# Second mixture of experts: parts of the work at the joins placed inside the branches, the down matmuls with 512 columns, the weight splits on VectorE in halves

## Chip, cores and metric

The kernel runs on one core of a Trainium2 chip. The metric is the device time of one execution in microseconds, lower is better; the median of several runs is quoted. The engines are named as in the profile: PE (TensorE, its weight loads are PEld), DVE (VectorE), ACT (ScalarE), POOL (GpSimd) and SP (SyncE, which issues most of the transfers). A name with a q behind it, as ACTq, is the engine's sequencer, with its branches and semaphore instructions.

## The reference

Three stages, in float32. A chunked linear attention gives 3072 rows of 256. Then two mixtures of experts follow, of which the change touches the second:

```python
# first mixture: 4 experts, every token goes through all of them
out += p[:, e:e+1] * (relu(x @ w1[e]) @ w2[e])           # w1: 256x1024, w2: 1024x256

# second mixture: 8 experts, each token goes to one, 768 places for each expert
expert_idx = argmax(x @ w_gate, axis=1)
gate_w = softmax(x @ w_gate)[token, expert_idx]
h = relu(disp[e] @ w1[e])                                # disp[e]: the tokens of expert e, in their order
y = h @ w2[e]
out[i] = gate_w[i] * y[expert_idx[i], pos[i]]            # 0 for a token that found no place
```

With the inputs of the measurement the experts get 836 (of which 768 have a place), 313, 184, 362, 215, 164, 196 and 802 (768) tokens.

## The kernel before

Attention, first mixture and routing are interleaved by hand up to about 607 us. The routing writes each token's row, with its gate and its index behind the 256 values, to `disp` in HBM, at its place in its expert. From there the second mixture runs expert by expert; it is this part that the change edits.

**Precision.** A float32 product is made of three matmuls: each operand is split into a high part in fp32r and the rest (h and l in the names), and h·h, h·l and l·h are summed in PSUM. For weights, `split_w` does it: ACT copies a stage of 128x1024 to the high part (L371), and DVE or POOL subtracts it to get the low part (L372). An expert has four such stages, c = 0 to 3, two for w1 and two for w2.

**A block.** `expert_block` runs one block of n = 256 (NARROW) or 384 (SLOTS) tokens of an expert, two or three token tiles of 128. For f = 0 to 7 the up part (`up_part`, L725 to L727) makes 128 of the 1024 hidden values for all n tokens in six matmuls; ACT puts relu of it into `ring_hh` (L729), and DVE the rest into `ring_hl` (L730). The ring has three such pairs. Two f's later (LAG) the down part takes the pair, for each token tile with three matmuls of 256 columns, into one PSUM tile per token tile (L763 to L765). At the block's end ACT scales each sum by the gate (`yo`, L773), and POOL scatters it to `out` by an indirect DMA (L774). Between the steps `go()` runs what the caller has put into `extra`: loading the next expert's rows, transposing them (`turn`, L695, with a copy of the gates, `gi`, on POOL, L697), splitting the transposed rows (`turned`, L703 and L704), loading weight stages and splitting the weights of expert e + 2, at steps 4, 6, 8 and 10. The splits of c = 1, 2 are on DVE, those of c = 0, 3 on POOL.

**The order of the experts.** The counts of tokens are read into registers, and `tc.If` chooses on every engine. For expert 0 the block of 384 always runs, and a second block if it has more than 384 tokens. For each further expert `head(e)`, the up part of f = 0, 1, 2 for the first 256 tokens (18 matmuls), is written ahead of the branches, since every choice has it. Behind it come a branch that runs a block of 256 (`wide{e}`, taken for up to 256 tokens), and one (`over{e}`) that holds a block of 384 (`full{e}`) and a pair of blocks (`next{e}`). At the end of a branch each engine raises the semaphores by what the path that was not chosen would have raised, so that what comes behind counts the same on both paths; the rows of L1090, L1093 and L1097 on the engines' sequencers are the branches and these updates. [...] Expert 7 has its Ifs nested, and behind it stands `redo_first`, a repetition of expert 0's block for other counts, which does not run here (L1063).

So the blocks that run are 384 + 384 for experts 0 and 7, 384 for 1 and 3, and 256 for 2, 4, 5 and 6: 26 token tiles.

```python
for e in range(1, E2):
    tokens = counts[e]
    head(e)
...
    with tc.If(tokens <= NARROW, label=f"wide{e}", preferred_fallthrough_block=True):   # L1090
        hint(f"over{e}")
        first_block(e, NARROW)
    with tc.If(tokens > NARROW, label=f"over{e}", preferred_fallthrough_block=True):    # L1093
```

## Time and profile before

| | us |
|---|---|
| median of 3 runs | 791.07 (789.83 to 792.62) |
| the profiled execution | 795.09 |
| its span, from the first to the last instruction | 793.3 |
| PE busy | 766.5 (97%) |
| DVE, ACT, POOL busy | 440.8 (56%), 282.9 (36%), 189.0 (24%) |
[...]

A span is what the profiler saw of one execution; the profiled execution's own time is 1.8 us longer, and 4.0 us over the median of the runs. Matmuls are pipelined, and the time shown for one is modelled, longer than the distance to the next one's start; idle time ahead of a matmul is counted from the modelled end of the one before. The granted clock is the share of full speed that the chip gave to PE.

### The profile page before, as it was taken

How to read it: one execution, taken by the hardware profiler on the slowest of the kernel's cores; microseconds unless marked ns; L12 is line 12 of the kernel's file. 1: busy time of each engine (PE TensorE's matmuls, PEld its weight loads, DVE VectorE, ACT ScalarE, POOL GpSimd, SP SyncE). 2: the span in 40 equal slices, each digit the busy share in tenths (PEclk: the TensorE clock that was granted, in tenths of full speed). 3: DMA queues.
4: the chain of work that ended last, by engine and by line, in shares of the span. 5: the costliest groups of instructions: out<-in, count | busy, mean ns of one | idle time of the engine just before them, and what ended most of it. 6: DMA issues, size and time to landing. Idle time of an engine off the chain costs nothing. (4 is left out here: it accounts for less than half of the span.)

```text
span 793.3 us, 13459 instructions
## 1 busy us (share of the span) xinstructions
PE 766.5 (97%) x5114; PEld 685.7 (86%) x5114; DVE 440.8 (56%) x884; ACT 282.9 (36%) x555; POOL 189.0 (24%) x227
## 2 busy tenths in 40 slices
PE   8999999999999999999999999999999989998996
PEld 7889999988878888888888888889999989897995
DVE  5886778457754577645666456543444323546321
ACT  2542543232323332233332323322453334555331
POOL 1010102212111122110221103011765313654211
PEclk9999999999999999999999999999999999999999
DMA  9753567523220232201322112040353214453100
GB/s 261 246 174 104 183 213 226 165 84 103 80 83 14 71 110 83 83 14 67 111 84 83 46 52 96 14 143 12 117 163 107 75 44 144 141 169 109 43 21 23
DMA packets 50195, 82.54 MB, mean 104 GB/s; under 512 B 5104, under 2 KB 35009, under 8 KB 50108
## 3 DMA queue, kind: packets, MB, share of 16 engines
q1 hardware_dynamic: 46340, 74.50, 30.0%
q0 software_dynamic: 2400, 6.11, 2.1%
q10 hardware_dynamic: 1368, 0.81, 0.4%
q8 instruction: 50, 0.82, 0.4%
q14 instruction: 37, 0.30, 0.1%
HBM read 65.56 MB, written 16.31 MB: 103 GB/s over the span
## 5 line engine op out<-in xcount | busy, mean ns | idle before, releaser
L502 DVE SCALAR_TENSOR_TENSOR hl<-ph,hh 128x512 fp32r<-128x512 f32 (+2 forms) x216 | 133.9, 620 | 221.7 <-ACT hh L501 218.1
L501 ACT ACTIVATE hh<-ph 128x512 fp32r<-128x512 f32 (+2 forms) x216 | 117.4, 543 | 348.4 <-PE ph L498 337.6
L496 PE MATMUL ph<-xh,w1h 128*128 128x512 f32 (+2 forms) x432 | 160.7, 372 | 1.6 <-DVE hl L502 1.6
L525 PE MATMUL acc<-hh,w2h 128*128 128x512 f32 (+2 forms) x432 | 158.1, 366 | 2.3 <-DVE x L541 1.4
L497 PE MATMUL ph<-xl,w1h 128*128 128x512 f32 (+2 forms) x432 | 156.4, 362 | 0.0
L498 PE MATMUL ph<-xh,w1l 128*128 128x512 f32 (+2 forms) x432 | 156.4, 362 | 0.0
L526 PE MATMUL acc<-hl,w2h 128*128 128x512 f32 (+2 forms) x432 | 156.3, 362 | 0.0
L527 PE MATMUL acc<-hh,w2l 128*128 128x512 f32 (+2 forms) x432 | 156.1, 361 | 0.0
L525 PEld LDWEIGHTS acc<-hh,w2h 128*128 128x128 f32 x432 | 81.2, 188 | 13.9 <-DVE x L541 2.2
L496 PEld LDWEIGHTS ph<-xh,w1h 128*128 128x128 f32 x432 | 81.3, 188 | 12.5 <-DVE hl L502 2.3
L730 DVE SCALAR_TENSOR_TENSOR ring_hl<-qh,ring_hh 128x384 fp32r<-128x384 f32 (+2 forms) x82 | 38.5, 472 | 95.8 <-ACT ring_hh L729 88.3
L498 PEld LDWEIGHTS ph<-xh,w1l 128*128 128x128 f32 x432 | 81.2, 188 | 10.5
L527 PEld LDWEIGHTS acc<-hh,w2l 128*128 128x128 f32 x432 | 81.3, 188 | 10.4
L526 PEld LDWEIGHTS acc<-hl,w2h 128*128 128x128 f32 x432 | 81.3, 188 | 9.4
L497 PEld LDWEIGHTS ph<-xl,w1h 128*128 128x128 f32 x432 | 81.3, 188 | 8.7
L549 POOL TENSOR_TENSOR x<-x,cmb 128x512 f32<-128x512 f32 (+2 forms) x40 | 48.5, 1234 | 153.0 <-DVE cmb L546 152.9
L729 ACT ACTIVATE ring_hh<-qh 128x384 fp32r<-128x384 f32 (+2 forms) x82 | 34.9, 425 | 83.8 <-PE qh L727 81.0
L765 PE MATMUL yy<-w2h,ring_hl 128*128 128x256 f32 x208 | 59.8, 287 | 0.0
L763 PE MATMUL yy<-w2h,ring_hh 128*128 128x256 f32 x208 | 59.7, 287 | 0.0
L764 PE MATMUL yy<-w2l,ring_hh 128*128 128x256 f32 x208 | 59.7, 287 | 0.0
L180 DVE TENSOR_TENSOR_SCAN lt<-abc,id 128x512 f32<-128x512 f32 x44 | 57.4, 1304 | 0.0
L725 PE MATMUL qh<-sxh,w1h 128*128 128x256 f32 (+2 forms) x132 | 42.0, 318 | 10.8 <-DVE ring_hl L730 3.0
(166 smaller groups left out, 1080.8 us busy)
## 6 DMA issues: line engine op xcount, KB each, us to landing
stg<-in_w SPq DMA_DIRECT2D x34, 512.0 KB
abc<-a_zero SPq DMA_DIRECT2D x21, 512.0 KB
bcr<-in_bc SPq DMA_DIRECT2D x19, 512.0 KB
disp<-zrow SPq DMA_DIRECT2D x12, 516.0 KB
nat<-in_nat SPq DMA_DIRECT2D x24, 256.0 KB
pb<-pT SPq DMA_DIRECT2D x16, 256.0 KB
rw<-disp SPq DMA_DIRECT2D x10, 387.0 KB
out<-zrow SPq DMA_DIRECT2D x6, 512.0 KB
```

The source lines that it names most:

```text
L180: nc.vector.tensor_tensor_scan(t["lt"][:, sl, :].rearrange("p h i -> p (h i)"), a_bc[:, sl, :].rearrange("p h i -> p (h i)"), id4.rearrang ...
L496: nc.tensor.matmul(ph[:, :n], lhsT=wh[:, c], rhs=xh[:, k, :n], start=k == 0, stop=False)
L497: nc.tensor.matmul(ph[:, :n], lhsT=wh[:, c], rhs=xl[:, k, :n], start=False, stop=False)
L498: nc.tensor.matmul(ph[:, :n], lhsT=wl[:, c], rhs=xh[:, k, :n], start=False, stop=k == KD - 1)
L501: nc.scalar.activation(hh[:, :n], ph[:, :n], AF.Relu)
L502: nc.vector.scalar_tensor_tensor(hl[:, :n], ph[:, :n], 0.0, hh[:, :n].bitcast(F32), ALU.max, ALU.subtract)
L525: nc.tensor.matmul(a[:, :n], lhsT=wh[:, c], rhs=hh[:, :n], start=f == 0, stop=False)
L526: nc.tensor.matmul(a[:, :n], lhsT=wh[:, c], rhs=hl[:, :n], start=False, stop=False)
L527: nc.tensor.matmul(a[:, :n], lhsT=wl[:, c], rhs=hh[:, :n], start=False, stop=f == NF - 1)
L763: nc.tensor.matmul(y[st], lhsT=hh[:, q], rhs=w2h[:, c], start=j == 0, stop=False)
L764: nc.tensor.matmul(y[st], lhsT=hh[:, q], rhs=w2l[:, c], start=False, stop=False)
L765: nc.tensor.matmul(y[st], lhsT=hl[:, q], rhs=w2h[:, c], start=False, stop=j == NF - 1)
```

## The change

- **Down part.** `w2h` and `w2l` become one tile `w2` of 128 x 2 x 2048. For each token tile and f a matmul of 512 columns multiplies `ring_hh` with both parts, into a PSUM tile of 128 x 2 x 256, and one of 256 columns adds `ring_hl` times the high part to its first half. At the end ACT scales the first half, and DVE adds the second half times the gate (L798), ahead of the scatter. Three such PSUM tiles are made once and used in rotation.
- **Splits.** In the second mixture's blocks all weight splits go to DVE, in halves of 512 columns, at steps m and m + 1.
- **gi.** The copy of gates and indices goes from POOL to DVE, in two instructions at the end of `turned`.
- **Joins.** `head(e + 1)` is no longer in front of the branches but written into every path that leads there, at the end or in the Else. Where the narrow branch isn't taken, its Else holds `first_down`: the down part of f = 0 and 1 for two token tiles. The repetition of expert 0 moves ahead of expert 1, its jump gets a hint ("again"), and expert 7's Ifs stand one behind the other.
- **Alignment.** JOIN becomes 0, and a slot of its own (FIRST_BLOCK) is given to expert 0's block.

```diff
@@ split_w
+    def split_w(moe, e, c, lo, part=slice(0, FF)):
...
+        sl = slice(FF * (c % 2) + part.start, FF * (c % 2) + part.stop)
+        st = given[moe, e, c][:, part]
         nc.scalar.copy(h[:, sl], st)
         lo.tensor_tensor(l[:, sl], st, h[:, sl].bitcast(F32), ALU.subtract)
@@ turn, turned
-        nc.gpsimd.tensor_copy(gi[e, k], rows[:, :, DM:ROW])
...
+        rows, g = whole["rows", e % 2 if k == 0 else 2], gi[e, k]
+        nc.vector.tensor_copy(g[:, :, 0:1], rows[:, :, DM:DM + 1])
+        nc.vector.tensor_copy(g.bitcast(I32)[:, :, 1:2], rows.bitcast(I32)[:, :, DM + 1:ROW])
@@ the down part
+    def down_part(e, y, q, j):
+        w2 = W[2, e][4]
+        hh, hl = ring[j % len(ring)]
+        c = slice(DM * j, DM * j + DM)
+        nc.tensor.matmul(y, lhsT=hh[:, q], rhs=w2[:, :, c], start=j == 0, stop=False)
+        nc.tensor.matmul(y[:, 0], lhsT=hl[:, q], rhs=w2[:, 0, c], start=False, stop=j == NF - 1)
...
+    def first_down(e, y):
+
+        for j in range(LAG):
+            for st, t in enumerate(y):
+                down_part(e, t, slice(P * st, P * st + P), j)
@@ expert_block
-                    nc.tensor.matmul(y[st], lhsT=hh[:, q], rhs=w2h[:, c], start=j == 0, stop=False)
-                    nc.tensor.matmul(y[st], lhsT=hh[:, q], rhs=w2l[:, c], start=False, stop=False)
-                    nc.tensor.matmul(y[st], lhsT=hl[:, q], rhs=w2h[:, c], start=False, stop=j == NF - 1)
+                    if st >= len(early[1]) or j >= lead:
+                        down_part(e, y[st], q, j)
...
-            nc.scalar.activation(o, y[st], AF.Copy, scale=g[:, st, 0:1])
+            nc.scalar.activation(o, y[st][:, 0], AF.Copy, scale=g[:, st, 0:1])
+            nc.vector.scalar_tensor_tensor(o, y[st][:, 1], g[:, st, 0:1], o, ALU.mult, ALU.add)
@@ first_block
-            add(m, lambda w=order[i], lo=(nc.vector if c in (1, 2) else nc.gpsimd): split_w(2, *w, lo))
+            add(m, lambda w=order[i]: split_w(2, *w, nc.vector, slice(0, FF // 2)))
+            add(m + 1, lambda w=order[i]: split_w(2, *w, nc.vector, slice(FF // 2, FF)))
@@ the branches
+    def choose(cond, label, yes, no):
+        with tc.If(cond, label=label, preferred_fallthrough_block=True) as choice:
+            yes()
+        if no:
+            with choice.Else():
+                no()
+
+    def full_program(e, tokens, y):
+        first_block(e, SLOTS, y, LAG, two=True)
+        second_into(e, tokens)
+        head(e + 1)
+        if e + 1 < E2:
+            align(JOIN)
+
+    def wide_programs(e, tokens, y, after):
...
+        choose(tokens <= SLOTS, f"full{e}", lambda: first_block(e, SLOTS, y, LAG, over=f"next{e}"), None)
+        choose(tokens > SLOTS, f"next{e}", lambda: full_program(e, tokens, y), after)
+
+    def narrow_program(e, y):
+        hint(f"over{e}")
+        first_block(e, NARROW, y, 0)
...
+        with tc.If(counts[0] > SLOTS, preferred_fallthrough_block=True):
+            hint("again")
+            second_into(0, counts[0])
+    choose(numbers["known"] < SLOTS, "again", first_once_more, lambda: head(1))
 
     for e in range(1, E2):
...
+        after = (lambda: head(e + 1)) if e + 1 < E2 else None
+        y = [sums(e, 0, st) for st in range(NARROW // P)]
+        choose(tokens <= NARROW, f"wide{e}", lambda: narrow_program(e, y), lambda: first_down(e, y))
+        choose(tokens > NARROW, f"over{e}", lambda: wide_programs(e, tokens, y, after), after)
```

**An expert's end on PE.** The place is the end of expert 1's second block. Before, the last down matmuls (yy; the columns are the row's number, the line, the operation, output and inputs, and the shape) are followed by the alignment (ISA) and the jumps, and then by expert 2's head (qh), which is there once, for all paths:

```order
3628 L763 MATMUL yy_1_2_7421<-w2h_1_5954,ring_hh_6304 128x256
3629 L764 MATMUL yy_1_2_7421<-w2l_1_5955,ring_hh_6304 128x256
3630 L765 MATMUL yy_1_2_7421<-w2h_1_5954,ring_hl_6305 128x256
3631 L785 ISA
3632 L1097 UNCONDITIONAL_BRANCH x2
3633 L1093 UNCONDITIONAL_BRANCH
3634 L725 MATMUL qh_0_0_7549<-sxh_5932,w1h_2_6134 128x256
```

Now the head comes directly behind the last down matmul of this path, with the alignment and the jump behind its 18 matmuls. Behind the jump the same 18 matmuls stand again, for the path without a second block:

```order
3606 L749 MATMUL yy_6377<-w_2_1_5947,ring_hh_6295 128x512
3607 L750 MATMUL yy_6377<-w_2_1_5947,ring_hl_6296 128x256
3608 L733 MATMUL qh_0_0_7611<-sxh_5925,w1h_2_6127 128x256
3609 L734 MATMUL qh_0_0_7611<-sxl_5926,w1h_2_6127 128x256
...
3624 L734 MATMUL qs_0_2_7629<-sxl_5926,w1h_2_6127 128x256
3625 L735 MATMUL qs_0_2_7629<-sxh_5925,w1l_2_6128 128x256
3626 L810 ISA
3627 L1080 UNCONDITIONAL_BRANCH
3628 L733 MATMUL qh_0_0_7639<-sxh_5925,w1h_2_6127 128x256
```

The head (qh, qs) moved from behind the paths' meeting to ahead of it, into each path, and three down matmuls became two.

**The splits on DVE in a narrow block.** Before, in expert 4's block of 256 tokens (ring_hl is L730, the split of the low parts of w1 and w2 L372, the turned rows L704):

```order
880 L730 SCALAR_TENSOR_TENSOR ring_hl_6301<-qh_0_3_9023,ring_hh_6300 128x256
881 L372 TENSOR_TENSOR w1l_2_6135<-stg_3_3_6243,w1h_2_6134 128x1024
882 L730 SCALAR_TENSOR_TENSOR ring_hl_6305<-qh_0_4_9040,ring_hh_6304 128x256
883 L372 TENSOR_TENSOR w2l_2_6137<-stg_4_0_6268,w2h_2_6136 128x1024
884 L730 SCALAR_TENSOR_TENSOR ring_hl_6309<-qh_0_5_9058,ring_hh_6308 128x256
885 L730 SCALAR_TENSOR_TENSOR ring_hl_6301<-qh_0_6_9085,ring_hh_6300 128x256
886 L704 TENSOR_TENSOR sxl_6299<-tr_0_0_9074,sxh_6298 128x384
```

And now in the same block:

```order
1045 L378 TENSOR_TENSOR w1l_2_6128<-stg_3_3_6235,w1h_2_6127 128x512
1046 L738 SCALAR_TENSOR_TENSOR ring_hl_6296<-qh_0_4_9125,ring_hh_6295 128x256
1047 L378 TENSOR_TENSOR w1l_2_6128<-stg_3_3_6235,w1h_2_6127 128x512
1048 L378 TENSOR_TENSOR w_2_2_6129<-stg_4_0_6260,w_2_2_6129 128x512
1049 L738 SCALAR_TENSOR_TENSOR ring_hl_6300<-qh_0_5_9143,ring_hh_6299 128x256
1050 L378 TENSOR_TENSOR w_2_2_6129<-stg_4_0_6260,w_2_2_6129 128x512
1051 L378 TENSOR_TENSOR w_2_2_6129<-stg_3_0_6091,w_2_2_6129 128x512
1052 L738 SCALAR_TENSOR_TENSOR ring_hl_6292<-qh_0_6_9169,ring_hh_6291 128x256
1053 L378 TENSOR_TENSOR w_2_2_6129<-stg_3_0_6091,w_2_2_6129 128x512
1054 L709 TENSOR_TENSOR sxl_6290<-tr_0_0_9159,sxh_6289 128x384
```

The two whole stages on DVE (and two on POOL) became eight halves on DVE, one or two of them between each ring_hl and the next.

**A block's end on DVE.** The yo additions (L798) now stand on DVE between the last ring_hl of a block (f = 7) and the first of the head, as here at expert 3's second block:

```order
1025 L738 SCALAR_TENSOR_TENSOR ring_hl_6296<-qh_1_7_8972,ring_hh_6295 128x384
1026 L798 SCALAR_TENSOR_TENSOR yo_1_0_8999<-yy_6376,gi_6284,yo_1_0_8999 128x256
1027 L798 SCALAR_TENSOR_TENSOR yo_1_1_9005<-yy_6377,gi_6284,yo_1_1_9005 128x256
1028 L798 SCALAR_TENSOR_TENSOR yo_1_2_9011<-yy_6375,gi_6284,yo_1_2_9011 128x256
1029 L738 SCALAR_TENSOR_TENSOR ring_hl_6292<-qh_0_0_9017,ring_hh_6291 128x256
1030 L738 SCALAR_TENSOR_TENSOR ring_hl_6296<-qh_0_1_9026,ring_hh_6295 128x256
```

Before, ring_hl of the head followed directly on ring_hl of f = 7, and yo was ACT's alone.

## Rows read from the trace of the kernel before

**Rows 1.** The page's first part: busy us, share of the span, instructions.

```profile
PE 766.5 (97%) x5114; PEld 685.7 (86%) x5114; DVE 440.8 (56%) x884; ACT 282.9 (36%) x555; POOL 189.0 (24%) x227
```

**Rows 2.** Two stretches: length, busy us and instructions of each engine, PEclk, DMA share, GB/s.

```profile
640.00:660.00 20.00, 17.57 (x122) 17.05 (x121) 5.53 (x11) 7.81 (x16) 5.42 (x5) 0.91 0.23 69
...
700.00:720.00 20.00, 17.00 (x130) 16.35 (x129) 10.59 (x14) 9.28 (x19) 8.87 (x6) 0.95 0.47 147
```

**Rows 3.** PE's waits, 607.6 to 786: releaser: us, times, longest.

```profile
PE qh L725 <- DVE ring_hl L730: 3.6, 4, 1.9
PE qh L725 <- ACTq L1093: 2.7, 4, 0.7
PE qh L725 <- DVEq L1090: 2.0, 2, 1.0
PE qh L725 <- ACTq L1097: 1.4, 2, 0.7
PE qh L725 <- ACT yo L773: 1.4, 1, 1.4
```

**Rows 4.** Timeline of PE at expert 0's end: start, length, operation, [idle before <-releaser].

```profile
645.43 0.28 PE L764 MATMUL yy<-w2l,ring_hh 128*128 128x256 f32 x1
645.55 0.28 PE L765 MATMUL yy<-w2h,ring_hl 128*128 128x256 f32 x1
647.25 0.36 PE L725 MATMUL qh<-sxh,w1h 128*128 128x256 f32 x1 [1.42 <-ACT yo L773]
```

**Rows 5.** Line L785: duration ns min/median/max, first and last start us.

```profile
L785 PEldq COMPARE_BRANCH  x1: 3011/3011/3011, 643.8 to 643.8; - x1
```

**Rows 6.** Line L1093, PE's sequencer, the same columns.

```profile
L1093 PEldq COMPARE_BRANCH  x6: 82/338/358, 649.8 to 747.2; - x6
```

**Rows 7.** Timeline of PE behind a wide branch and behind a join.

```profile
650.63 0.33 PE L725 MATMUL qh<-sxh,w1h 128*128 128x128 f32 x1 [0.99 <-DVEq L1090]
...
669.89 0.38 PE L725 MATMUL qh<-sxh,w1h 128*128 128x256 f32 x1 [0.75 <-ACTq L1097]
```

**Rows 8.** Groups of DVE, 640 to 785 (busy, mean ns), and one of its splits.

```profile
L730 DVE SCALAR_TENSOR_TENSOR ring_hl<-qh,ring_hh 128x256 fp32r<-128x256 f32 x34 | 14.2, 422 | 40.2 <-ACT ring_hh L729 34.6 <-issue 5.5
L704 DVE TENSOR_TENSOR sxl<-tr,sxh 128x384 fp32r<-128x384 f32 x12 | 6.1, 548 | 0.0
L730 DVE SCALAR_TENSOR_TENSOR ring_hl<-qh,ring_hh 128x128 fp32r<-128x128 f32 x9 | 2.6, 292 | 5.8 <-ACT ring_hh L729 5.7
...
692.90 1.23 DVE L372 TENSOR_TENSOR w1l<-stg,w1h 128x1024 fp32r<-128x1024 f32 x1 [0.38 <-ACT w1h L371]
```

**Rows 9.** Timeline of PE and ACT at the last matmul.

```profile
785.15 0.28 PE L765 MATMUL yy<-w2h,ring_hl 128*128 128x256 f32 x1
...
785.47 0.47 ACT L773 ACTIVATE yo<-yy,gi 128x256 f32<-128x256 f32 x1 [0.24 <-PE yy L765]
```

**Rows 10.** Timeline of PE, the first of 15 matmuls and the first behind them.

```profile
652.93 0.42 PE L763 MATMUL yy<-w2h,ring_hh 128*128 128x256 f32 x1
...
656.63 0.28 PE L763 MATMUL yy<-w2h,ring_hh 128*128 128x256 f32 x1
```

**Rows 11.** Timeline of PE in the first mixture, first and last of eleven matmuls.

```profile
299.64 0.39 PE L497 MATMUL ph<-xl,w1h 128*128 128x512 f32 x1
...
301.91 0.39 PE L527 MATMUL acc<-hh,w2l 128*128 128x512 f32 x1
```

**Rows 12.** Timeline of DVE, POOL and PE in expert 4's block.

```profile
712.79 3.36 DVE L372 TENSOR_TENSOR w2l<-stg,w2h 128x1024 fp32r<-128x1024 f32 x1
...
712.70 2.37 POOL L372 TENSOR_TENSOR w2l<-stg,w2h 128x1024 fp32r<-128x1024 f32 x1
...
716.54 0.39 PE L725 MATMUL qh<-sxh,w1h 128*128 128x256 f32 x1 [1.93 <-DVE ring_hl L730]
```

**Rows 13.** Timeline of PE at the second block of expert 0.

```profile
630.62 0.45 PE L725 MATMUL qh<-sh,w1h 128*128 128x384 f32 x1 [0.59 <-DVE ring_hl L730]
```

**Rows 14.** Timeline of POOL at the end.

```profile
787.39 0.98 POOL L774 DMA_INDIRECT out<-yo,gi  x1 [0.30 <-DMA out<-yo,gi]
```

## Prediction

> **What bounds the kernel now.** I read the busy shares first: TensorE (PE) is busy 97% of the span and no other engine over 56% [rows 1], so time can only come from PE's own work or from holes in it. Cutting the span into stretches shows where the holes are: in the second mixture, PE is busy 17.57 of 20 us between 640 and 660 and 17.00 between 700 and 720, and in the same two stretches its granted clock is 0.91 and 0.95 [rows 2]. The list of what PE waited for in 607.6 to 786 names thirteen waits [rows 3]: nine on a branch or a join between experts (ACTq L1093 four, ACTq L1097 two, DVEq L1090 two, and one that is put down to the yo of ACT), 7.5 us, and four on ring_hl of VectorE (DVE), 3.6 us. The change touches nothing ahead of the second mixture but the names of weight tiles and two small copies, so the sum is about the 178 us from 607.6 on.

> **The joins.** After expert 0's last matmul, issued at 645.55, PE starts nothing until 647.25 [rows 4]. The row blames ACT, but the branch on PE's own queue (L785) takes 3011 ns from 643.8 [rows 5], while the six branches of L1093 took at most 358 ns [rows 6]. Those of [rows 6] that jump far have a hint ahead of them, and the one of [rows 5] has none. The change puts a hint ("again") ahead of it, and the head of expert 1 behind it, inside the Else. Eight further holes have one shape: 0.99 us idle ahead of 650.63 at a wide branch, 0.75 ahead of 669.89 at a join [rows 7]. At the end of a branch each engine makes up by semaphore updates for the path that was not taken, and PE's next block waits for those of ACT or DVE, which come behind the rest of their previous block. The change moves head(e+1), 18 matmuls, ahead of that: PE has 18 × 0.12 = 2.16 us of work which needs only PSUM freed by an earlier ring_hl and the turned rows, not the yo. On the wide branch eight matmuls (first_down, 4 × (0.227 + 0.12) = 1.39 us) stand ahead in the same way. The cover is enough: a hole, end to start, is 0.75 to 1.4 us. What becomes late next is DVE, which has the yo additions ahead of the head's first ring_hl; the additions, at about 0.42 us (the ring_hl form of the same shape, [rows 8]), come one behind each token tile, and only the last lies behind PE's last matmul. The last yo of ACT starts 0.32 us after the last matmul and takes 0.47 [rows 9]; with the addition that is 1.2 us, and ring_hl of f=0, which needs its own 0.72 us of matmuls and ACT's hh as well (1.4 us), should be done 1.8 us after it, ahead of the 2.16 us at which first_down wants it.
> What goes: idle of 7.5 us [rows 3], plus 0.16 us for each of nine, because a modelled matmul lasts 0.28 us where the next one starts after 0.12 [rows 4]: 8.95 us. The first matmul after a hole is slower by some 0.1 us, which I leave in. [...] Together **−10.5**. Bounds: nothing regained of the clock (−8.9), and the second, smaller stretch at the low clock around 718 too (−11.6, by the 0.05 × 20 us of [rows 2]).

> **The narrow experts 2, 4 and 5.** Here the splits of expert e+2's weights compete with ring_hl. A DVE split of 1024 columns takes 1.23 us beside an idle POOL [rows 8], but 3.36 us when POOL splits at the same time, and ring_hl behind it then holds PE for 1.93 us [rows 12]. The change takes the POOL splits away and doubles those of DVE. Between ring_hl of f=3 and of f=7 DVE will do 8 halves × 0.65 (half of 1.23 and a little; an estimate from [rows 8]) = 5.2, five ring_hl × 0.42 = 2.1, two sxl × 0.55 = 1.1, two gi copies, each taken at half of the 0.29 us of the smallest form, 0.3: 8.7 us. PE needs, for five f's, six pairs of downs and six transposes, 5 × 0.72 + 12 × 0.347 + 6 × 0.12 = 8.5 us. DVE starts about a microsecond behind and has one pair of downs in reserve, 0.69 us: late by 8.7 + 1.0 − 8.5 − 0.69 = 0.5, and I take 0.65, since DVE also waits a little for ACT in between. In three experts that is 1.95 us, against 3.6 − 0.59 = 3.0 idle now [rows 3, 13], plus 3 × 0.26 for pitch and restart, plus about 1.1 at the lower clock between 700 and 740 (0.05 × 20 us of [rows 2] as the nearest): 4.9. So **−2.9**. Bounds: splits so quick that nothing is late (−4.9); 2.0 us each (+1.1). In experts 1 and 3, of three token tiles, PE has half as much work again and DVE is covered. ACT's casts in halves cost a few tenths per expert, beside other work.

> **Fewer, longer matmuls.** For each of 26 token tiles and 8 f's, two matmuls of 256 columns become one of 512. The down matmuls start every 0.12 us now, and those of 512 columns in the first mixture every 0.227 us, by the first and the last of eleven in a row [rows 11]: 208 × (0.24 − 0.227) = **−2.7**. Bounds: 0 (the two-part operand runs as two of 256) and −2.7.

> **What is added.** (a) The 26 yo additions on DVE, 0.42 each, lie behind a block's end; only at expert 0, where the second block follows with no head between, do they meet something: PE already waits there 0.59 us for ring_hl [rows 13], and three additions are queued ahead of the same ring_hl, of which one is not yet past: **+0.45** (bounds 0 and 1.3). (b) Expert 7 is now two Ifs in a row (full7, next7) in place of nested ones, with no head to cover the drain: a join as it stands now, 2.7 us in four [rows 3]: **+0.7** (bounds 0.5 and, with the stop of [rows 4] in addition, 2.1). (c) The gi copies on DVE: one waits for the scatters that used the same gi. They are a block or more old, so I cost the wait at nothing; if they were late, ring_hl of f=7 would be late by as much. (d) The end: yo is now ACT then DVE, +0.45 ahead of the last scatters, and the wait on L1063 between them goes (0.30 us idle is left ahead of the last scatter, [rows 14]): **0**, bounds −0.5 and +0.5.

> **Sum.** −10.5 − 2.9 − 2.7 + 0.45 + 0.7 = −14.95. The profiled execution took 795.09 us, with a span of 793.3; it is 4.0 us over the median of the runs, 0.5%, more than the runs differ among themselves, so I take the difference from the median: 791.07 − 14.95 = 776.1, and expect a profiled span near 778.4 (793.3 − 14.95). A difference under 0.3%, 2.4 us, could not be told from none.

> **Rivals.**
> 1. *DVE becomes the bound in narrow experts.* ring_hl of f=7 comes 2 us late three times: −2.9 turns into +1.1, and a low-clock stretch of 1.57 follows once: 776.1 + 4.0 + 1.6 = 781.7. For it: DVE's 8.7 us against PE's 8.5. Against: without POOL beside it each split is short [rows 8].
> 2. *The joins stay* with another name: the head's first matmuls wait for the drain after all, because the updates stand in its own instructions. Half of the 8.95 us and all of the 1.57 stay: 776.1 + 6.1 = 782.2. All of both: 786.6.
> 3. *Slower: fetches.* Every jump to another place in PE's program stops as in [rows 5], its hint or alignment having moved. Each costs 1.58 us of hole (1.42 idle + 0.16), and at most 1.57 more at the low clock: about 3.1. It decides from five misses on (14.95 / 3.1 = 4.8); nine, one for each of the old holes, give 776.1 + 28 = 804. For it: the program's order of Ifs, hints and alignment all change. Against: the hinted jumps are quick now [rows 6], and the change keeps the hint ahead of each and adds one. [...]
> 4. *The 512-column matmul is no cheaper.* w2h and w2l lie 2048 columns apart, and the engine reads them as two runs: the 2.7 stays, 778.8. No matmul of the trace has such an operand, for or against; the 512 columns of [rows 11] are one run.

> **How the numbers follow.** My forecast 0.62, rival 1 0.15, rival 2 0.08, rival 3 0.05, rival 4 0.10. The forecast alone covers 772 to 780 by the bounds: −2.0 for the narrow experts and −1.1 for the clock at the low end; +1.3 at expert 7, +0.9 at expert 0 and +1.6 for the clock at the high end. The range of 8 in 10 takes in rivals 1 and 4 and half of rival 2: 771.5 to 783.5. Faster by over 0.3% in all cases but the third, and a little off for all that could stack up: 0.92 faster, 0.04 within 0.3%, 0.04 slower.

> **What would show it.** In the profile after: PE busy 98% or more of a span of about 778; of the nine waits on a branch or join only one of 0.7 us or so at expert 7; no L785-like branch of 3 us; splits of 128x512 on DVE near 0.65 us and none on POOL after 640; the down matmul of 512 columns starting 0.227 us ahead of the next; ring_hl waits at experts 2, 4 and 5 of some 0.65 us. I am wrong if PE shows waits of 1 us or more on DVE's L738 or L798 at the joins, if a branch of 3 us recurs, or if PE's clock stays low in a stretch of more than 2 us.

## The result, and the profile after

The changed kernel takes **780.2 us** (median of 4 runs, 778.62 to 780.54), the kernel before 790.7 in the same comparison (789.83 to 792.62). The ratio is 0.9866, 95% interval [0.9843, 0.989]; a second comparison on another chip gave 781.51 against 792.94 and 0.985 [0.981, 0.989]. The forecast was 776.1, with a range of 771.5 to 783.5: the sign and the range held, and the gain, 10.5 us, is 4.4 us short of the 14.95 that were summed up.

The profiled executions differ by more, 793.3 to 776.8 us of span. First part of the page, to be held against [rows 1], of the changed kernel:

```profile
PE 759.9 (98%) x4906; PEld 671.6 (86%) x4906; DVE 461.3 (59%) x960; ACT 285.0 (37%) x575; POOL 157.5 (20%) x207
```

The two stretches of [rows 2] (same columns; the same work lies a little earlier now):

```profile
640.00:660.00 20.00, 19.93 (x129) 18.65 (x129) 10.68 (x21) 9.88 (x23) 2.95 (x3) 1.00 0.29 89
700.00:720.00 20.00, 19.59 (x139) 18.07 (x137) 17.07 (x36) 14.96 (x34) 1.96 (x2) 1.00 0.51 154
```

PE is busy nearly throughout, at full clock, and DVE is busy for 10.7 and 17.1 us where it was for 5.5 and 10.6. What PE waits for in the second mixture, against [rows 3]:

```profile
PE yy L750 <- DVE ring_hl L738: 1.2, 3, 0.4
PE qh L733 <- DVE ring_hl L738: 1.0, 1, 1.0
PE cps L561 <- PE pos L624: 0.4, 1, 0.4
PE qh L733 <- PEq L1080: 0.3, 1, 0.3
```

All nine waits on branches and joins are gone; the one of L1080 is expert 7's. Three on ring_hl are the narrow experts 2, 4 and 5, one is expert 0's second block. The row of cps lies in expert 0's first block and is not in a second trace of the changed kernel. In the timeline of PE, expert 0's end, where 1.42 us of idle stood [rows 4], now reads:

```profile
645.43 0.40 PE L749 MATMUL yy<-w,ring_hh 128*128 128x512 f32 x1
645.67 0.28 PE L750 MATMUL yy<-w,ring_hl 128*128 128x256 f32 x1
645.79 0.28 PE L733 MATMUL qh<-sxh,w1h 128*128 128x256 f32 x1
```

The head starts 0.12 us behind the last down matmul. The same timeline holds the three places where something is left, expert 2's end, expert 7's branch and expert 0's second block:

```profile
676.38 0.39 PE L750 MATMUL yy<-w,ring_hl 128*128 128x256 f32 x1 [0.41 <-DVE ring_hl L738]
...
737.80 0.32 PE L733 MATMUL qh<-sxh,w1h 128*128 128x128 f32 x1 [0.32 <-PEq L1080]
...
630.93 0.44 PE L733 MATMUL qh<-sh,w1h 128*128 128x384 f32 x1 [0.96 <-DVE ring_hl L738]
```

And in the groups of DVE from 640 to 775, a split of 512 columns takes 0.69 us where 0.65 was estimated, and an addition to yo 0.48 where 0.42 was:

```profile
L378 DVE TENSOR_TENSOR w1l<-stg,w1h 128x512 fp32r<-128x512 f32 x20 | 13.4, 688 | 1.1 <-ACT w1h L377 0.4 <-DMA rw<-disp 0.2
L378 DVE TENSOR_TENSOR w<-stg,w 128x512 fp32r<-128x512 f32 x20 | 13.3, 689 | 0.2
L798 DVE SCALAR_TENSOR_TENSOR yo<-yy,gi,yo 128x256 f32<-128x256 f32 x23 | 11.1, 484 | 13.0 <-ACT yo L797 13.0
```

### The profile page after: what moved, and what is told of

It is laid out like the page before. It is cut to its first block, busy times and chain, and to the rows that moved or that the text cites. A ratio compares the mean times of both kernels' runs of the same rounds, so it can differ in the third digit from the quotient of the medians.

```text
span 776.8 us, 13171 instructions
## 1 busy us (share of the span) xinstructions
PE 759.9 (98%) x4906; PEld 671.6 (86%) x4906; DVE 461.3 (59%) x960; ACT 285.0 (37%) x575; POOL 157.5 (20%) x207
## 5 line engine op out<-in xcount | busy, mean ns | idle before, releaser
L531 PE MATMUL acc<-hh,w 128*128 128x512 f32 (+2 forms) x432 | 158.1, 366 | 2.3 <-DVE x L547 1.4
L532 PE MATMUL acc<-hl,w 128*128 128x512 f32 (+2 forms) x432 | 156.3, 362 | 0.0
L533 PE MATMUL acc<-hh,w 128*128 128x512 f32 (+2 forms) x432 | 156.1, 361 | 0.0
L531 PEld LDWEIGHTS acc<-hh,w 128*128 128x128 f32 x432 | 81.2, 188 | 14.0 <-DVE x L547 2.2
L504 PEld LDWEIGHTS ph<-xh,w1l 128*128 128x128 f32 x432 | 81.2, 188 | 10.5
L533 PEld LDWEIGHTS acc<-hh,w 128*128 128x128 f32 x432 | 81.3, 188 | 10.4
L532 PEld LDWEIGHTS acc<-hl,w 128*128 128x128 f32 x432 | 81.3, 188 | 9.4
L749 PE MATMUL yy<-w,ring_hh 128*128 128x512 f32 x208 | 76.5, 398 | 0.0
L738 DVE SCALAR_TENSOR_TENSOR ring_hl<-qh,ring_hh 128x384 fp32r<-128x384 f32 (+2 forms) x82 | 38.7, 473 | 52.5 <-ACT ring_hh L737 51.6
L750 PE MATMUL yy<-w,ring_hl 128*128 128x256 f32 x208 | 58.6, 282 | 1.2 <-DVE ring_hl L738 1.2
L799 POOL DMA_INDIRECT out<-yo,gi x26 | 25.5, 980 | 128.9 <-DVE yo L798 125.5
L749 PEld LDWEIGHTS yy<-w,ring_hh 128*128 128x128 f32 x208 | 39.1, 188 | 6.1
```

The source lines that it names most:

```text
L504: nc.tensor.matmul(ph[:, :n], lhsT=wl[:, c], rhs=xh[:, k, :n], start=False, stop=k == KD - 1)
L531: nc.tensor.matmul(a[:, :n], lhsT=wh[:, c], rhs=hh[:, :n], start=f == 0, stop=False)
L532: nc.tensor.matmul(a[:, :n], lhsT=wh[:, c], rhs=hl[:, :n], start=False, stop=False)
L533: nc.tensor.matmul(a[:, :n], lhsT=wl[:, c], rhs=hh[:, :n], start=False, stop=f == NF - 1)
L749: nc.tensor.matmul(y, lhsT=hh[:, q], rhs=w2[:, :, c], start=j == 0, stop=False)
L750: nc.tensor.matmul(y[:, 0], lhsT=hl[:, q], rhs=w2[:, 0, c], start=False, stop=j == NF - 1)
```

## Experiments

The kernels were run in groups, each beside runs of the kernel before; across groups only ratios to before are compared. The pitch is the distance from one matmul's start to the next one's in an undisturbed row; a wait "over the pitch" is what a start comes later than that.

### Both kernels once more

No edit. The question was the 4.4 us between the profiled execution of before and its median.

> The kernel before, once more, for a second trace. The profiled run of before took 795.09 us, 4.4 over the median of its runs. [...] Rival: the part ahead of the second mixture differs by 4 us from run to run, and the second mixture is as in the first trace (177.5 us from its first to its last matmul).

> The changed kernel, once more, for a second trace beside the one of before. Theory 1: second mixture of 162.9 us from its first to its last matmul, as in the first trace (607.49 to 770.31), 780 us in all, any difference to the 776.8 us span of the first trace lies in a stretch at the lower clock or at the end. Rival: the part ahead of the second mixture is longer.

Measured: 793.39 and 781.51 us, before 792.94. The three parts of the four traces, in us (start of the second mixture's first up matmul, from there to the start of the last matmul, from there to the end):

| | first part | second mixture | end |
|---|---|---|---|
| before | 607.60 | 177.55 | 8.15 |
| before_again | 605.89 | 176.16 | 7.83 |
| after | 607.49 | 162.66 | 6.68 |
| after_again | 608.85 | 165.00 | 6.69 |

Against this rival stood a usual run with the same nine waits, a part ahead of 607 us that differs by no more than 0.3 us, less low clock and a shorter end. Neither holds alone: all three parts vary. The second mixture of before_again has the same nine waits, to 0.1 us, but no stretch at the low clock in 640 to 660, and one in 700 to 720 that is deeper:

```profile
640.00:660.00 20.00, 17.69 (x134) 17.17 (x133) 6.74 (x12) 9.12 (x17) 7.33 (x6) 1.00 0.31 96
700.00:720.00 20.00, 16.30 (x118) 15.27 (x117) 9.57 (x12) 9.18 (x19) 10.71 (x8) 0.91 0.47 143
```

The first part differs in its first 15 us. Eight matmuls of the opening last 2.09 us in after_again and 1.14 in after, and the sixteen behind them 1.92 and 1.06; after_again is 1.4 us behind from there to the start of the second mixture:

```profile
5.10 2.09 PE L851 MATMUL spread<-spare,ones 1*128 1x512 f32 x8 [0.69 <-DVE spare L887]
```

Nine of the twelve traces of changed kernels have the long form, and their second mixture starts at 608.8 to 609.4 us; the three with the short form start it at 607.4 to 607.5. Neither of the two of before has the long form. Those two differ in another thing: PE's granted clock is 0.50 from 9 to 11 us in before and 1.00 in before_again. Whether the change has a part in the long form (it renames the tiles there) was not tried, and two traces of before are few.

In the second mixture after_again loses 2.3 us more than after, at experts 2 and 4, and there ACT is the first to be late. Its relu of the head's third part starts 2.1 us after PE has finished it, where ACT idled 0.28 us ahead of it in the first trace (timelines of ACT, of after_again and then of after):

```profile
667.48 0.39 ACT L737 ACTIVATE ring_hh<-qh 128x256 fp32r<-128x256 f32 x1 [0.24 <-PE qh L735]
670.18 0.39 ACT L737 ACTIVATE ring_hh<-qs 128x256 fp32r<-128x256 f32 x1 [2.32 <-PE qh L735]
...
666.87 0.39 ACT L737 ACTIVATE ring_hh<-qs 128x256 fp32r<-128x256 f32 x1 [0.28 <-PE qs L735]
```

DVE's splits then start later too. They catch up in part, and at the end of these two experts PE idles 0.85 us for ring_hl of f = 7 in place of 0.41.

### The splits on two engines again

```diff
-            add(m, lambda w=order[i]: split_w(2, *w, nc.vector, slice(0, FF // 2)))
-            add(m + 1, lambda w=order[i]: split_w(2, *w, nc.vector, slice(FF // 2, FF)))
+            add(m, lambda w=order[i], lo=(nc.vector if c in (1, 2) else nc.gpsimd): split_w(2, *w, lo))
```

> The changed kernel with the weight splits of its blocks as before: whole stages of 1024, c = 1, 2 on VectorE and c = 0, 3 on POOL. My theory (the splits slow each other on the two engines): ring_hl waits in experts 2, 4 and 5 return, 3 to 5 us more than the changed kernel, 783 to 785 us; a split of 1024 on VectorE takes 2.3 to 3.4 us there. Rival (the splits were never the limit, the joins were all): within 1 us of the changed kernel.

Measured: 787.97, against 781.51 of after_again in the same group: 6.5 us. The theory holds and its size was too small. The waits on ring_hl come to 8.8 us, more than the 3.6 of before [rows 3], and a split of w2 on DVE takes 2.46 us in the mean:

```profile
L378 DVE TENSOR_TENSOR w<-stg,w 128x1024 fp32r<-128x1024 f32 x5 | 12.3, 2456 | 0.0
```

The likely reason is that the holes at the joins had been time in which DVE caught up; without them the late ring_hl costs twice as much. The additions to yo, which DVE does here and did not do before, are not the reason: joins_only_b below is without them and still waits 7.4 us.

### Three matmuls of 256 columns again

```diff
-        nc.tensor.matmul(y, lhsT=hh[:, q], rhs=w2[:, :, c], start=j == 0, stop=False)
+        nc.tensor.matmul(y[:, 0], lhsT=hh[:, q], rhs=w2[:, 0, c], start=j == 0, stop=False)
+        nc.tensor.matmul(y[:, 0], lhsT=hh[:, q], rhs=w2[:, 1, c], start=False, stop=False)
...
-            nc.vector.scalar_tensor_tensor(o, y[st][:, 1], g[:, st, 0:1], o, ALU.mult, ALU.add)
```

> The changed kernel with the down part as three matmuls of 256 columns and without VectorE's addition to yo. My theory: 2.0 to 2.7 us more on PE's matmuls and up to 0.5 us less at expert 0 (no additions ahead of ring_hl) and 0.5 less at the end: 1 to 2 us slower than the changed kernel, 781 to 782. Rival (a two-part operand of 512 columns costs as much as two of 256): 0.5 to 1 us faster than the changed kernel.

Measured: 801.02, 19.5 us over the changed kernel and 8 over the one before (ratio to before 1.01 [1.0061, 1.0139]). Neither theory had that. PE's waits ("issue" is a wait for nothing that the profile shows) and one place of its timeline show it:

```profile
PE qh L733 <- issue: 12.3, 5, 4.0
PE yy L751 <- DVE ring_hl L738: 1.9, 3, 0.8
```

```profile
679.25 0.28 PE L751 MATMUL yy<-w,ring_hl 128*128 128x256 f32 x1
683.58 0.55 PE L733 MATMUL qh<-sxh,w1h 128*128 128x256 f32 x1 [4.04 <-issue]
```

The branches behind the four narrow experts take 3.1 to 4.6 us on PE's sequencer, where no branch of the changed kernel takes over 0.44 (line L1080 of three_256, and then of after):

```profile
L1080 PEldq COMPARE_BRANCH  x30: 72/222/4586, 645.4 to 791.6; - x30
```

```profile
L1080 PEldq COMPARE_BRANCH  x30: 72/192/436, 644.3 to 768.5; - x30
```

```diff
-JOIN = 0
+JOIN = 217
```

> [...] Then here no branch of PE takes over 0.5 us and the time is 782 to 785 us; what is left over the changed kernel is the price of three matmuls. [...]

Measured: 781.15, ratio 0.9884 [0.9822, 0.9947] where three_256 had 1.01: over 2% by one number. The jumps of the narrow experts are quick again, at most 0.45 us, with as many instructions as in three_256. So the slot decides, and not their number; how it does so was not shown. The theory's sign, no branch over 0.5 us, did not come: three others, near the start of experts 1, 2 and 4, take 1.9 to 2.4 us, of which PE waits 0.6 us in all. And the matmuls' price is at last to be seen: the ratio is within the changed kernel's own interval, so in all they are worth nothing that these runs can tell. By the trace there is a little: 512 columns start 0.233 us ahead of the next in the median and the 256 behind them 0.117, 0.350 together against 0.36 for three of 256: 208 × 0.010 = 2 us gained. The additions that came with them take back 0.4 us at expert 0 (0.75 over the pitch without them, 1.13 with) and 0.5 at the end (6.17 against 6.68).

### The 512 columns in one run

```diff
...
-        nc.tensor.matmul(y, lhsT=hh[:, q], rhs=w2[:, :, c], start=j == 0, stop=False)
-        nc.tensor.matmul(y[:, 0], lhsT=hl[:, q], rhs=w2[:, 0, c], start=False, stop=j == NF - 1)
+        nc.tensor.matmul(y, lhsT=hh[:, q], rhs=w2[:, j], start=j == 0, stop=False)
+        nc.tensor.matmul(y[:, 0], lhsT=hl[:, q], rhs=w2[:, j, 0], start=False, stop=j == NF - 1)
```

> The changed kernel with w2's high and low part of one f side by side, so that the 512 columns lie in one run, with the weight splits writing runs of 256. If two runs cost PE something (the 512-column matmuls of the changed kernel start 0.2325 us ahead of the next in the median, those of the first mixture 0.2275): 208 x 0.005 = 1 us less. Rival: it is the same 0.2325 here, and the time is within 0.5 us of the changed kernel.

Measured: 781.51, ratio 0.9889 [0.9828, 0.995]: no change that shows, and in the groups of PE the same mean to the nanosecond (398, of after and then of one_run):

```profile
L749 PE MATMUL yy<-w,ring_hh 128*128 128x512 f32 x208 | 76.5, 398 | 0.0
...
L754 PE MATMUL yy<-w,ring_hh 128*128 128x512 f32 x208 | 76.5, 398 | 0.0
```

Two runs cost nothing: the pitch is 0.232 us here and 0.2325 there. What the 5 ns over a row of equals (0.2275) come from was not shown; the shorter matmul behind gets 3 of them back (0.117 for 0.12).

### The joins as before

The branches of before (head ahead of them, nested Ifs for expert 7, JOIN 8) around everything else of the change:

```diff
...
     for e in range(1, E2):
         tokens = counts[e]
-        after = (lambda: head(e + 1)) if e + 1 < E2 else None
...
+        head(e)
...
```

> The branches as before (head ahead of the branches, nested Ifs for expert 7, the repetition of expert 0 at the end, JOIN 8), with the 512-column matmuls, VectorE's yo additions, the gi copies and the halved splits of the change. Theory: the nine waits on branches and joins are back (9 us start to start, longer by up to 0.4 each where VectorE's addition is what the join waits for), and with them some low clock: 790 to 795 us. Rival (the splits brought most of it): under 785 us.

Measured: 795.12, ratio **1.0042** [1.0014, 1.007]: with the other parts of the change, and without the joins, the kernel is slower than before. PE's waits of old_joins:

```profile
PE qh L732 <- DVEq L1122: 6.0, 4, 1.5
PE qh L732 <- DVEq L1126: 3.1, 2, 1.5
PE qh L732 <- DVEq L1119: 2.0, 2, 1.0
```

Six joins of 0.7 [rows 3] have become six of 1.5, since DVE's last addition stands behind ACT's yo and is what they wait for now. In the changed kernel the same additions run beside the head. The ninth wait, behind expert 0, is not back: the branch there has no hint, as before, but takes 317 ns and not the 3011 of [rows 5]:

```profile
L809 PEldq COMPARE_BRANCH  x1: 317/317/317, 645.6 to 645.6; - x1
```

So a missing hint alone does not make a slow branch. In this trace the second mixture takes 175.8 us, no more than before (177.6 and 176.2): against the longer joins stand the shorter matmuls, waits on ring_hl of 2.3 us in place of 3.6, and the missing ninth wait. The first part (609.3, with the long opening) and the end (9.2) are what is longer here. The loss of 0.4% is thus not shown to be one of the second mixture.

### The joins alone

The edits of pool_splits and three_256_b together: of the change, only the branches, the small gi copies on DVE and the common tile of w2 are left, with JOIN at 217.

> [...] Theory: the joins alone are worth what they cost before, 10 to 12 us, and the narrow experts' waits stay as in pool_splits (7 us of excess): 784 to 788 us, near pool_splits. Rival: without the additions on VectorE the joins gain nothing over pool_splits but the matmuls cost 2.1 us more: 789 us or more.

Measured: 787.31, ratio 0.9952 [0.9934, 0.9971]. The theory's number holds, its reason only in part: the joins are gone, and PE waits for ring_hl instead:

```profile
PE qh L733 <- DVE ring_hl L738: 7.4, 6, 1.9
PE qh L733 <- PEq L1079: 0.3, 1, 0.3
```

So the joins alone bring 0.5% and the rest alone costs 0.4%; together they bring 1.3 to 1.5%. The traces, in which the first part can be left out, say the same of second mixture and end: 7 to 9 us less than in the two of before with the joins alone, none with the rest alone (184.9 against 185.7 and 184.0), 12 to 16 with both. Neither half can be priced by itself.

### Without the new hint

```diff
-            hint("again")
```

> The changed kernel without its new hint "again", ahead of the one jump that had none before. Theory: the jump to expert 1's head takes about 3 us on PE's queue again, 1.4 to 2.2 us of idle PE, now ahead of the head instead of behind, and perhaps a stretch at the low clock: 1.5 to 3.5 us slower than the changed kernel, 783 to 785. [...]

Measured: 784.45, ratio 0.9913 [0.9887, 0.9938], by the ratios 4 to 5 us over the changed kernel, a little more than expected. The jump is the one of [rows 5] again (line L1080), and PE idles ahead of the head (timeline of PE):

```profile
L1080 PEldq COMPARE_BRANCH  x30: 72/201/3344, 645.3 to 773.3; - x30
```

```profile
648.84 0.36 PE L733 MATMUL qh<-sxh,w1h 128*128 128x256 f32 x1 [1.86 <-DVE yo L798]
```

The row blames DVE, as that of [rows 4] blamed ACT. This confirms the reading of [rows 4, 5], and that the slow branch costs 2.0 us there (1.86 of idle and 0.16 of pitch); what else of the 4 to 5 us is due to it was not separated.

### A faster version

```diff
...
-            m, i = (4, 6, 8, 10)[c], 4 * (e + 2) + c
+            m, i = (2, 4, 6, 8)[c], 4 * (e + 2) + c
...
+        if e == E2 - 1:
+            choose(tokens > SLOTS, f"next{e}", lambda: full_program(e, tokens, y), lambda: first_block(e, SLOTS, y, LAG))
+            return
```

> The changed kernel with two edits: expert 7's two wide cases as If and Else of one branch, and the weight splits two steps earlier (m = 2, 4, 6, 8). Theory: no drain at expert 7 (0.72 us), no wait on ring_hl at the end of experts 2, 4 and 5 (0.6 to 1.0 us each): 2 to 3.5 us faster than the changed kernel, 777 to 779 us. Rival: the splits, earlier, hold up ring_hl of f = 3 and 4 instead, and the waits only move: 780.5.

Measured: **777.57**, ratio 0.984 [0.9776, 0.9904]. By the ratios that can't be told from the changed kernel's, but in the same group one_run and three_256_b, which take what the changed kernel takes, stand at 781.5 and 781.2, all of their runs slower than all of this kernel's. Both kinds of wait are gone; what remains is expert 0's wait, and two of 0.2. What each of the two edits brings was not separated:

```profile
PE qh L733 <- DVE ring_hl L738: 1.2, 2, 1.0
PE cps L561 <- PE pos L624: 0.2, 1, 0.2
```

To this, expert 0's yo was deferred: passed on as a list and run from the second block's steps 1 and 2, in the Else otherwise.

```diff
...
+            second_into(0, counts[0], {1: left[:1], 2: left[1:]})
+        with two.Else():
+            for p in left:
+                p()
```

> nest_early, and the yo of expert 0's first block put behind ring_hl of f = 0 and 1 of its second block, on ACT, VectorE and POOL alike. Theory: of the 1.13 us that PE loses at the start of that block nearly all goes: 0.8 to 1.1 us faster than nest_early, 776.5 us. Rival: the wait moves to the second block's f = 2, whose PSUM tile is freed by the same late ring_hl: no gain.

Measured: 778.7, ratio 0.983 [0.9807, 0.9853], which can't be told from nest_early; these two are the fastest kernels. The wait it was meant for fell from 1.13 to 0.33 us over the pitch, as the theory has it. But at the join into expert 5 DVE stood still for 2.5 us, with ACT's input there since 711.46, and PE lost 2.1 us (timeline of DVE). DVE's sequencer shows no instruction at all from a branch at 710.91 to its next semaphore wait at 713.62:

```profile
710.72 0.48 DVE L798 SCALAR_TENSOR_TENSOR yo<-yy,gi,yo 128x256 f32<-128x256 f32 x1 [0.18 <-ACT yo L797]
713.70 0.75 DVE L738 SCALAR_TENSOR_TENSOR ring_hl<-qh,ring_hh 128x256 fp32r<-128x256 f32 x2 [2.50 <-ACT ring_hh L737]
```

The last kernel asked whether these pauses of ACT and DVE are late instructions:

```diff
-        tc.mark_branch_hint_location(label, "LikelyTaken", engines=[mybir.EngineType.PE])
+        tc.mark_branch_hint_location(label, "LikelyTaken", engines=[mybir.EngineType.PE, mybir.EngineType.Activation, mybir.EngineType.DVE])
```

> nest_early with the branch hints given to ACT and VectorE as well as to PE. Theory: in the second trace of the changed kernel ACT stood still for 2.0 us ahead of the third relu behind the joins into experts 2 and 4 (668.1 to 670.2, 700.9 to 702.9) though PE had its input ready, and not in the first trace; ACT's own instructions came late behind a jump. With hints none of these relus starts over 0.6 us behind its input, in this trace and so in most runs: 1 to 2 us faster than nest_early in the median, 775.5 to 776.5 us. Rival: the pause does not come from the jump's fetch, and the hints change nothing (777.5).

Measured: 787.15, ratio 0.9906 [0.9871, 0.9941]: 0.7% over nest_early, whose interval it meets, and clear of best1's. The pause is still there, 3.0 us at expert 2 on ACT, and DVE has one like it inside expert 4's block; PE idles 2.7 and 2.8 us for them (PE's waits, then the timeline of ACT):

```profile
PE yy L750 <- DVE ring_hl L738: 2.8, 1, 2.8
PE yy L749 <- ACT ring_hh L737: 2.7, 1, 2.7
...
669.91 0.66 ACT L737 ACTIVATE ring_hh<-qh 128x256 fp32r<-128x256 f32 x2 [3.19 <-issue]
```

Here too ACT's sequencer shows nothing from a branch at 666.64 to 669.76. The pauses are without any instruction, in other places and longer with the hints (3.0 us on ACT, 2.1 in after_again). That they are instructions that come late was the author's estimate, and no trace shows it; neither theory predicted a slower kernel, and the cause of the pauses stays open.

## Why the prediction held, and where it was off

**The joins (−10.5).** The mechanism is right in each point: the head covers all of them, ring_hl comes in time, and the low clock is gone (1.00 from 640 to 770 us). The hint does away with the 3 us, as no_hint shows (3344 ns without it, at most 436 with it); but old_joins has neither the hint nor the 3 us (317 ns), so the hint is needed for this layout and not for every one. As a price of the joins by themselves the −10.5 was wrong: joins_only_b gives 0.5%, not 1.3%, and PE's waits on ring_hl grow from 3.6 to 7.4 us, as with the holes gone DVE has less time. Only in the sum with the splits does it come out. The 1.57 us of low clock in the sum are 3.70 us for the 15 matmuls of [rows 10], behind expert 1's wide branch, less 2.13, an estimate from the starts of [rows 4, 11] (9 × 0.12 + 6 × 0.175, midway between 0.12 and 0.227); the mean granted clock there is 0.54. This was in part luck: the second trace of before does not have the stretch (1.00 in 640 to 660).

**The narrow experts (−2.9).** Three waits of 0.58 us over the pitch were left in the first trace where 0.65 was taken; in the second trace two were 1.02, with 0.5 to 0.6 more ahead of them in the same two experts, behind ACT's pauses, which the step did not have. The step was priced against before, where the joins still gave slack: undoing it alone costs 6.5 us.

**The matmuls (−2.7).** Sized too large: 2 us, for 512 columns take 0.233 us here, not the 0.227 of a row of equals. Rival 4's reason, that an operand in two runs costs more, is refuted by one_run (0.232 us in one run, 0.2325 in two). Its outcome, that nothing is gained, can't be excluded by the runs: three_256_b, with three matmuls, takes 781.15 us beside the 781.51 of one_run, since the additions that come with the 512 columns take back about half of what PE gains.

**What is added.** Expert 0: 0.38 for 0.45. Expert 7: 0.48 and 0.24 behind it, 0.72 for 0.7. Both right. **The end (0, −0.5 to +0.5) is the step that failed**: its change lies outside the step's own bounds, for it is 1.5 and 1.1 us shorter in the two pairs of traces. The step counted POOL's wait ahead of the last scatter and overlooked the one behind it: with the If of L1063 gone, POOL's closing drain starts at once, beside the scatters' transfers, which go on to 774.9 us, and not behind them. In old_joins, where this If is back, the end takes 9.2 us, and in the other changed kernels 6.1 to 6.8 (the drain of before, then of after):

```profile
L1153 POOLq DRAIN  x3: 46/107/1547, 790.9 to 793.0; - x3
```

```profile
L1181 POOLq DRAIN  x3: 51/112/3480, 772.3 to 776.6; - x3
```

**The sum.** Second mixture and end come to −16.4 us in the pair of traces on which the prediction stood, and to −12.3 in the second pair: 14.3 in the mean, near the 14.95. That hides a difference of 4 us between the pairs. Before loses 1.4 us less in its second mixture the second time, with the same nine waits, and the changed kernel 2.3 more, by ACT's pauses; the prediction took one execution of before, longer than all four that were timed, for typical, and gave the changed kernel no pauses. The execution that was profiled after is the shortest of its four. The sum also put the part ahead of the second mixture at nothing. It is 3.0 us longer in the second pair, and nine of twelve changed kernels have the long opening there. If most runs have it, 1 to 3 us of the 4.4 lie in it, an estimate from the starts of 608.8 to 609.4 against 605.9 and 607.6; how the 4.4 us divide is not settled. That the time fell into the range owes something to the width that was given for other things.

**The rivals.** The first (DVE becomes the bound) describes such a run in part. The second did not come. The third did not come in the changed kernel, but three_256 is that rival: four branches of 3.1 to 4.6 us, and 801 us. The prediction looked for it at jumps without a hint; the four have theirs. The change rests on its slot, JOIN, as much as on its new order; the forecast gave that 1 in 20 without asking at which slot the narrow experts' branches stand.

## What to carry to other kernels

A hole on the bounding engine was slack for the others here (waits on ring_hl of 3.6 us with the holes, 7.4 without): price the parts of a change together, or undo each in the finished version, since here one half alone gained 0.5% and the other nothing of a joint 1.4%. After any change of the number of instructions between a hint and its jump, look at each branch's own duration on its sequencer, not at the releaser that the idle row names: one constant for a slot made 781 us of 801 here. Take a second trace of the kernel before the sum, and look at its untouched part too: what varies between two traces belongs in the range and not in the sum.

## What was not expected of the hardware

ACT or DVE pauses for 1.1 to 3.1 us with its input ready (2.1 on ACT in after_again, 2.2 on DVE in best1, 3.0 on ACT in hints_all), nearly always behind a join into a narrow expert, in nine of the twelve traces of changed kernels, and in one of two traces of the same kernel; the kernel with hints on their queues has the longest. And eight matmuls of the opening last either 1.14 or 2.09 us, in two traces of the same kernel too, which the whole program then carries. Neither cause was found.
